# A long-convolution kernel: row turning cut in quarters, two backward steps moved together, bank copies shared with VectorE, loads placed at two points of a slot

## The chip, the cores and the metric

The kernel runs on 1 core of one Trainium2 chip. The metric is device time in microseconds (us) of one launch. Before the change the median of 3 runs is 559.1 us (557.64 to 561.18). The execution that the profiler recorded took 559.32 us; the span from its first to its last instruction is 557.5 us, so 1.8 us lie around the span. All instants below are us from the start of that span.

## What is computed

For one sequence of L = 2048 positions and D = 512 channels, all in float32:

```python
xn = _layernorm(x, axis=-1)
s = _A_ref(xn, ...)                       # a causal long convolution per channel, plus a skip term
g = _silu(_B_ref(xn, w1, b1, w2, b2))     # FFN 512 -> 1792 -> 512 with GELU, then SiLU
return x + s * g
```

`_A_ref` builds a convolution kernel K of length 2048 for each channel from 128 complex modes, and convolves it with the normalised rows by Fourier transforms:

```python
P = jnp.exp(logdA[:, :, None] * l[None, None, :])
K = jnp.einsum("dn,dnl,dn->dl", Cc, P, dB).real
...
y = irfft2(rfft2(up) * rfft2(Kp))[..., :L] + u * Dskip
```

## The kernel before

**Two phases.** The first phase (until 408.32 us) holds the layer norm, both FFN matrix products (each operand split in a high and a low part, three products each), and the generation of the convolution kernels. Its order is the long string `ORDER`, and the change does not reorder it. Nearly all of the change lies in the second phase, the convolution. Its order is written out by hand too: for each of 4 blocks of 128 channels (`b` = 0 to 3) the function `slot(b, g)` is called for `g` = 0 to 7. Every engine takes its instructions strictly in the order in which `slot` and its callees issue them; nothing reorders them later.

**One block.** A transform of 2048 points is taken as 32 by 64.

- `first_dft(b, u, h, gs)` (line 879, matmul L887) is the first forward step of half `h` of the channels, for the rows (`u` = 0) or the convolution kernel (`u` = 1). It writes four PSUM banks. Each of its 64 matrix instructions in the trace is small. `first_out` (L893) copies the four banks into the tile `X` of the next block.
- `second_dft(b, g)` (L907) is the second forward step for 4 of the 32 frequencies, in a PSUM tile of its own tag (two buffers). `spectrum` (L915) copies the rows' half of it to SBUF (`uh`), `product` (L924) multiplies it with the kernel's half, and `combine` (L932, L934, every second slot) makes the complex product `Y` (two buffers).
- `back_dft(b, j)` (L943) is the first backward step for the frequencies of slots 2j and 2j+1. It fills two banks, which `back_out` (L954) copies into `Z`. `turn(b, kh, s)` (L963) transposes a half of `Z` into `T` on VectorE.
- `last_dft` (L983) is the last backward step of a whole block in four banks. `last_out` multiplies with the gate on VectorE (L990) and adds x on GpSimd (L991), and `store` writes four pieces to `out`.

**Banks.** `bank()` hands out four general PSUM banks in turn (two of tag `c`, two of tag `a`). A bank comes free when the copy that reads it is done, so the fifth bank asked for waits for the copy of the first.

**Pipelining between blocks.** While block `b` is in slots 0, 2, 4, 6, its slot also runs the four `first_dft` calls of block `b + 1`: slots 0 and 2 for the rows, 4 and 6 for the kernel. The last parts of a block run in the slots of the next one: the fourth backward step in slot 1, the turns in slots 0 to 4, `last_dft` and `last_out` in slot 5 (slot 4 of the last block).

**The raw rows.** The normalised rows lie in DRAM (`xs`). `side_piece` (L837) loads them for block `b + 2` in four pieces into the tile `raw`; the elements come with the channel innermost. `side_turn` (L856) copies `raw` to `in` with the channel outermost. It does so in two halves on ScalarE in slot 7, one before `spectrum` and one between `spectrum` and `back_out`. `raw`, turned rows and kernel rows share one tag of two buffers, so the kernel rows of block `b + 1` (`kernel_load`, `kernel_half`, L872, two halves of 512 KB) can be loaded once the raw rows are turned; before the change they come at the ends of slots 0 and 1. `side_skip` adds the skip term to each half on GpSimd (L877) before `first_dft(.., 1, ..)` reads it in slots 4 and 6.

**Loads.** All loads of this phase go out on SyncE, in order. `pace` (L799) is a small memset on VectorE into the tile to be loaded; the load waits for it, so a load starts no sooner than VectorE reaches that point of its order. `tail_load` (L972) brings a quarter of the gate and of x.

**The end.** After the loop the last backward step and `last_dft` of block 3 run in halves; for each half of the positions VectorE multiplies (L1145, L1148), one engine adds x (L1149), and two stores go out (L994).

## Time and profile before

| what | value |
|---|---|
| median of 3 runs | 559.1 us (557.64 to 561.18) |
| profiled execution | 559.32 us, span 557.5 us, mean granted TensorE clock 0.989 |
| busy: TensorE matmul, VectorE, ScalarE, GpSimd | 534.6, 454.1, 401.0, 279.8 us |
| first phase | 0 to 408.32 us |
| blocks 0, 1, 2, 3 | from 408.32, 439.72, 478.34, 516.19 us |
| after the loop | 545.19 to 557.5 us |
| moved by DMA | 85.89 MB, mean 154 GB/s |

How to read it: a row of the timeline gives the start and the length in us, the engine, the line, the operation, the names `out<-in`, the size, and how many instructions were merged into the row; in brackets stands the idle time of that engine ahead of it and what ended it. Successive matmuls overlap, so the time that a group really takes is read from its start to the start of the next group. A row of the windows view gives a stretch, its length, the busy time and instruction count of TensorE matmul, weight load, VectorE, ScalarE and GpSimd, then the granted share of the TensorE clock, the busy share of the DMA engines and GB/s.

### The profile page before, as it was taken

The page shows a single profiled execution, that of the slowest core. Times are in us where ns is not written, and L with a number is a line of the kernel's source. Part 1 is how long each engine was busy: PE and PEld are TensorE (multiplying, and loading weights), DVE is VectorE, ACT ScalarE, POOL GpSimd, SP SyncE. Part 2 cuts the span into 40 slices and gives each one's busy share as a digit, 9 for nine tenths or more (in the row PEclk, how much of TensorE's full clock was granted, in tenths as well). Part 3 has the DMA queues.
Part 4 walks back from the last instruction along what each step waited for, and adds up shares of the span by engine and source line. Part 5 has one row for each costly group of instructions (what it writes and reads, how often), then busy time and mean ns, then how long its engine had stood idle before and what let it go on. Part 6 is the DMA issues. An engine that isn't in the chain of part 4 may idle for free.

```text
span 557.5 us, 17629 instructions
## 1 busy us (share of the span) xinstructions
PE 534.6 (96%) x7511; PEld 427.4 (77%) x7511; DVE 454.1 (81%) x720; ACT 401.0 (72%) x580; POOL 279.8 (50%) x383
## 2 busy tenths in 40 slices
PE   8898999999999999999999999999999999999993
PEld 7666777778777777777777777777789887898971
DVE  6899999999999789998897876897453666466996
ACT  3687998799977999869798787799265752743430
POOL 5657389459776579969843484463110003003032
PEclk9999999999999999999999999999998999899998
DMA  8946535835292264834249126442468275362552
GB/s 223 301 151 218 174 127 171 259 127 195 57 325 92 84 220 107 292 105 104 40 133 295 54 91 92 133 115 95 163 232 172 61 236 72 108 200 77 164 198 101
DMA packets 88396, 85.89 MB, mean 154 GB/s; under 512 B 42263, under 2 KB 65051, under 8 KB 87293
## 3 DMA queue, kind: packets, MB, share of 16 engines
q1 hardware_dynamic: 79248, 66.40, 40.2%
q0 software_dynamic: 8768, 17.83, 10.5%
q8 instruction: 59, 0.97, 0.7%
q10 hardware_dynamic: 300, 0.53, 0.3%
q14 instruction: 21, 0.16, 0.1%
HBM read 51.18 MB, written 33.55 MB: 152 GB/s over the span
## 4 chain that ended last, share of the span: by engine, by line
PE 72%; DVE 19%; issue 3%; ACT 2%; DMA 1%; POOL 1%; DVEq 0%; ACTq 0%; SPq 0%; POOLq 0%
PE s L907 10%; PE z L287 8%; PE z L288 7%; PE z L289 7%; PE f L248 7%; PE f L250 7%; PE f L249 7%; PE s L887 6%; PE sa L943 5%; PE kg L655 5%; PE ph L591 2%; DVE hl L274 2%; DVE ra L605 2%; DVE e L644 2%; DVE e L640 1%
## 5 line engine op out<-in xcount | busy, mean ns | idle before, releaser
L617 POOL TENSOR_TENSOR mm<-mm,rc 128x32 f32<-128x32 f32 (+4 forms) x150 | 115.0, 766 | 11.8
L287 PE MATMUL z<-w2h,hh 128*128 128x512 f32 x224 | 97.8, 437 | 0.0
L248 PE MATMUL f<-xh,w1h 128*128 128x512 f32 x220 | 91.4, 415 | 0.0
L289 PE MATMUL z<-w2h,hl 128*128 128x512 f32 x224 | 88.5, 395 | 0.3 <-DVE hl L274 0.3
L250 PE MATMUL f<-xh,w1l 128*128 128x512 f32 x220 | 87.1, 396 | 1.7 <-DVE w1l L233 1.7
L288 PE MATMUL z<-w2l,hh 128*128 128x512 f32 x224 | 88.6, 396 | 0.0
L249 PE MATMUL f<-xl,w1h 128*128 128x512 f32 x220 | 86.7, 394 | 0.0
L924 DVE TENSOR_TENSOR t<-s,uh 128x512 f32<-128x512 f32 x64 | 41.0, 682 | 42.3 <-ACT uh L915 42.0
L907 PE MATMUL s<-X,mc 64*64 64x128 f32 x1536 | 63.7, 282 | 0.1
L274 DVE TENSOR_TENSOR hl<-hf,hh 128x512 fp32r<-128x512 f32 x56 | 53.2, 954 | 4.4 <-ACT hh L268 4.4
L614 POOL COPY mm<-rc 128x32 f32<-128x32 f32 x30 | 13.3, 443 | 78.1 <-DVE e L647 53.4
L907 PEld LDWEIGHTS s<-X,mc 64*64 64x64 f32 x1536 | 47.8, 138 | 5.5 <-DVE t L924 1.7
L250 PEld LDWEIGHTS f<-xh,w1l 128*128 128x128 f32 x220 | 41.3, 188 | 12.8 <-DVE w1l L233 3.0
L262 ACT ACTIVATE hf<-f,b1s 128x512 f32<-128x512 f32 x56 | 38.2, 688 | 17.7 <-DVE hl L274 10.1
L289 PEld LDWEIGHTS z<-w2h,hl 128*128 128x128 f32 x224 | 42.1, 188 | 11.0 <-DVE hl L274 1.1
L287 PEld LDWEIGHTS z<-w2h,hh 128*128 128x128 f32 x224 | 42.5, 190 | 10.3 <-issue 1.0
L605 DVE SCALAR_TENSOR_TENSOR ra<-ra,ph 128x512 f32<-128x512 f32 x64 | 43.6, 681 | 8.3 <-ACT ra L599 7.3
L248 PEld LDWEIGHTS f<-xh,w1h 128*128 128x128 f32 x220 | 41.5, 189 | 9.4 <-issue 0.3
L288 PEld LDWEIGHTS z<-w2l,hh 128*128 128x128 f32 x224 | 42.3, 189 | 8.2 <-DVE w2l L233 0.2
L249 PEld LDWEIGHTS f<-xl,w1h 128*128 128x128 f32 x220 | 41.4, 188 | 9.1
L640 DVE TENSOR_TENSOR e<-mm,ra 128x1024 f32<-128x1024 f32 x32 | 42.9, 1341 | 5.0 <-ACT ra L628 2.6
L893 ACT COPY X<-s 128x512 f32<-128x512 f32 x52 | 27.1, 597 | 25.0 <-PE s L887 25.0
(184 smaller groups left out, 1160.5 us busy)
## 6 DMA issues: line engine op xcount, KB each, us to landing
x<-in_A_u_dram SPq DMA_DIRECT2D x8, 512.0 KB
xs<-x SPq DMA_DIRECT2D x8, 512.0 KB
xt_h<-xh POOLq DMA_DIRECT2D x4, 1024.0 KB, 5.5
xt_l<-xl POOLq DMA_DIRECT2D x4, 1024.0 KB, 7.5
kgd<-ko SPq DMA_DIRECT2D x32, 128.0 KB
za<-zo SPq DMA_DIRECT2D x4, 1024.0 KB
xh<-xt_h POOLq DMA_DIRECT2D x4, 1024.0 KB, 6.1
xl<-xt_l POOLq DMA_DIRECT2D x4, 1024.0 KB, 9.9
```

What stands on the lines that cost most here:

```text
L248: PE.matmul(p, wh[:, k, :], xh[:, k, :], start=(k == 0), stop=False)
L249: PE.matmul(p, wh[:, k, :], xl[:, k, :], start=False, stop=False)
L250: PE.matmul(p, wl[:, k, :], xh[:, k, :], start=False, stop=(k == KD - 1))
L274: V.tensor_sub(hl, hf, hh)
L287: PE.matmul(z, hh[:, s], wh, start=(f0 == 0 and not rows), stop=False)
L288: PE.matmul(z, hh[:, s], wl, start=False, stop=False)
L289: PE.matmul(z, hl[:, s], wh, start=False, stop=(f0 == FA - 1))
L605: V.scalar_tensor_tensor(ra[:, 0, c], ra[:, 1, c], MAGIC, p, op0=ALU.subtract, op1=ALU.subtract)
L617: GP.tensor_mul(mv[:, :, 0:3:2, w:2 * w], mv[:, :, 0:3:2, 0:w], rc[:, 2 + 2 * i:4 + 2 * i, :].rearrange("p j c -> p c j").unsqueeze(3).to_ ...
L640: V.tensor_mul(e1, m1.unsqueeze(1).to_broadcast([P, 2, CH, N1]), ra[:, :, :, :N1])
L907: PE.matmul(p[ka * 64:(ka + 1) * 64, r, o, :, jj], w, xf[b][h, c, :, k, :], start=(c == 0), stop=(c == 1), skip_group_check=True)
L924: V.tensor_mul(t, p[:, i, :, 1].unsqueeze(1).to_broadcast([P, 2, 2, P]), uh)
```

## The change

1. `side_turn` works in quarters of the channels instead of halves. For block `b + 2` quarter 0 stands in slot 7 of block `b` ahead of `spectrum`, quarter 1 in the same slot behind `back_out`, quarters 2 and 3 in slots 0 and 1 of the next block, behind that slot's copies. The two calls outside the loop copy four quarters in one go.
2. `back_dft` of a middle block (1, 2): the second one moves from slot 6 to slot 7, the third one from slot 7 to slot 1 of the next block, where it stands directly ahead of the fourth. `back_out` now stands right behind `spectrum`.
3. `first_out`: VectorE takes two of the four bank copies in every even slot of block 0 (before: none) and in slots 4 and 6 of blocks 1 and 2 (before: slot 4 alone), and one in slots 0 and 2 of blocks 1 and 2 (before: none). VectorE's copies stand behind `product`.
4. Loads stand at two places of a slot (`loads(b, g, 0)` ahead of `product`, `loads(b, g, 1)` at the end), by a table. The kernel rows move from slots 0 and 1 to slots 2 and 3, the tails from slots 0, 1, 2 to places in slots 0, 1, 2, and the raw rows keep slots 3 to 5.
5. The first turn of blocks 0 to 2 moves from slot 7 to slot 0 of the next block, the second from slot 0 to slot 1. In the last block a turn moves from slot 3 to slot 2, and `last_out` of block 2 moves ahead of `product`.
6. At the end, in each half of the positions GpSimd adds one half of the channels and VectorE the other (before: GpSimd both in the first half of the positions, VectorE both in the second).

```diff
--- before.py
+++ after.py
@@ -843,16 +843,16 @@
 
     raws = {}
 
-    def side_turn(b, hs=(0, 1), eng=A):
+    def side_turn(b, qs=range(4), eng=A):
         if b not in raws:
             if b:
                 t = SB["pf"].tile([P, DB, N2], F32, tag="in", name=f"in0_{b}", bufs=2)
             else:
                 t = wka.tile([P, DB, N2], F32, tag="xl", name="in0_0", bufs=2)
-            raws[b] = side[b].rearrange("p m d -> p d m")
+            raws[b] = t, side[b].rearrange("p m d -> p d m")
             side[b] = [[t[:, :DB // 2], t[:, DB // 2:]]]
-        for h in hs:
-            d, r = side[b][0][h], raws[b][:, h * DB // 2:(h + 1) * DB // 2]
+        for q in qs:
+            d, r = (t[:, q * DB // 4:(q + 1) * DB // 4] for t in raws[b])
             A.copy(d, r) if eng is A else eng.tensor_copy(d, r)
 
     def kernel_load(b):
@@ -862,7 +862,7 @@
         else:
             k = [wka.tile([P, DB // 2, N2], F32, tag="x", name=f"in1_0_{h}", bufs=2) for h in range(2)]
         side[b].append(k)
-        for h in range(2 if b < 2 else 0):
+        for h in range(2 if b < 2 else 1):
             kernel_half(b, h)
 
     def kernel_half(b, h):
@@ -887,10 +887,11 @@
                 PE.matmul(p[:, i, :], src[r, 2 * i:2 * i + 2, :], fc[r], start=True, stop=True, skip_group_check=True)
         fp[b, u, h] = list(zip(gs, ps))
 
-    def first_out(b, u, h, engs=(A, A, A, A)):
-        for n, (g, p) in enumerate(fp.pop((b, u, h))):
-            d, p = xf[b][:, :, u, :, 16 * g + 8 * h:16 * g + 8 * h + 8], p.rearrange("p i (c k) -> p c k i", c=2)
-            A.copy(d, p) if engs[n] is A else engs[n].tensor_copy(d, p)
+    def first_out(b, u, h, engs=(A, A, A, A), only=None):
+        for n, (g, p) in enumerate(fp[b, u, h]):
+            if only in (None, engs[n]):
+                d, p = xf[b][:, :, u, :, 16 * g + 8 * h:16 * g + 8 * h + 8], p.rearrange("p i (c k) -> p c k i", c=2)
+                A.copy(d, p) if engs[n] is A else engs[n].tensor_copy(d, p)
 
     sp, sm, yy = {}, {}, {}
 
@@ -993,44 +994,78 @@
     def store(b, t, q):
         q.dma_start(out[b, t], gx[b][1][:, t * TB:(t + 1) * TB].rearrange("p q m -> p (q m)"))
 
+    def loads(b, g, late):
+        def tails(b, *ts):
+            for t in ts:
+                tail_load(b, t)
+
+        def raw(n):
+            if n == 0:
+                side[b + 2] = SB["pf"].tile([P, N2, DB], F32, tag="in", name=f"raw{b + 2}", bufs=2)
+            side_piece(b + 2, n)
+
+        if b == 0:
+            plan = {(1, 0): lambda: mc_load(2), (1, 1): lambda: ct_load(1), (2, 0): lambda: mc_load(3),
+                    (4, 1): lambda: ct_load(2), (6, 1): lambda: ct_load(3)}
+        elif b < NB - 1:
+            plan = {(0, 1): lambda: tails(b - 1, 0), (1, 0): lambda: tails(b - 1, 1), (1, 1): lambda: tails(b - 1, 2),
+                    (2, 0): lambda: kernel_load(b + 1), (2, 1): lambda: tails(b - 1, 3),
+                    (3, 0): lambda: kernel_half(b + 1, 1)}
+        else:
+            plan = {(0, 1): lambda: tails(b - 1, 0), (1, 0): lambda: tails(b - 1, 1), (1, 1): lambda: tails(b - 1, 2),
+                    (2, 0): lambda: tails(b - 1, 3)}
+            plan.update({(g, 1): lambda g=g: tails(b, g - 2) for g in range(2, 6)})
+        if b + 2 < NB:
+            order = ((3, 0), (3, 1), (4, 0), (5, 0)) if b == 0 else ((3, 1), (4, 0), (4, 1), (5, 0))
+            plan.update({k: lambda n=n: raw(n) for n, k in enumerate(order)})
+        if b == NB - 1 and b not in gx and g == 2:
+            big = SB["pf"].tile([P, 2, N1, P], F32, tag="X0", name="last")
+            gx[b] = big[:, 0, :NQ], big[:, 1, :NQ]
+        plan.get((g, late), lambda: None)()
+
     def slot(b, g):
         nxt = b + 1 < NB
         last = not nxt
         i = g // 2
-        sa = {3: (b, 0), 5: (b, 1), 7: (b, 2)}
+        sa = {3: [(b, 0)], 5: [(b, 1)], 7: [(b, 2)]}
         if b:
-            sa[1] = b - 1, 3
-        if b and nxt:
-            sa[6] = sa.pop(5)
-        sa = sa.get(g)
+            sa[1] = [(b - 1, j) for j in ((2, 3) if b > 1 else (3,))]
+            if nxt:
+                sa[7] = sa.pop(5)
+        sa = sa.get(g, [])
         end = b and g == 5 - last
         if b and nxt and g == 4:
             turn(b - 1, 1, 1)
         if last and g == 6:
             turn(b, 0, 0)
         second_dft(b, g)
-        if b + 2 < NB and g == 3:
-            side[b + 2] = SB["pf"].tile([P, N2, DB], F32, tag="in", name=f"raw{b + 2}", bufs=2)
-            side_piece(b + 2, 0)
-        if sa:
-            back_dft(*sa)
+        for k in sa:
+            back_dft(*k)
         if end:
             py = [bank(f"y{b - 1}_{n}").rearrange("p e m -> p (e m)") for n in range(G)]
             last_dft(b - 1, 0, py)
             last_dft(b - 1, 1, py)
-        if nxt and g % 2 == 0:
+        first = nxt and g % 2 == 0
+        if first:
+            engs = (A, A, V, V) if b == 0 or g > 2 else (A, A, A, V)
             first_dft(b + 1, i // 2, i % 2, range(G))
-        turning = b + 2 < NB and g == 7
-        if turning:
+        if b + 2 < NB and g == 7:
             side_turn(b + 2, (0,))
         spectrum(b, g)
-        if turning:
+        for k in sa:
+            back_out(*k)
+        if first:
+            first_out(b + 1, i // 2, i % 2, engs, A)
+        if b + 2 < NB and g == 7:
             side_turn(b + 2, (1,))
-        if sa:
-            back_out(*sa)
-        if nxt and g % 2 == 0:
-            first_out(b + 1, i // 2, i % 2, (A, A, V, V) if b and g == 4 else (A, A, A, A))
+        if nxt and b and g < 2:
+            side_turn(b + 1, (2 + g,))
+        if last and end:
+            last_out(b - 1, py)
+        loads(b, g, 0)
         product(b, g)
+        if first:
+            first_out(b + 1, i // 2, i % 2, engs, V)
         if last and g > 5:
             js = slice(2 * g - 12, 2 * g - 10)
             combine(b, 3, 1, js)
@@ -1038,40 +1073,19 @@
         elif g % 2:
             combine(b, i, 1)
             combine(b, i, 0)
-        if end:
+        if nxt and end:
             last_out(b - 1, py)
-        if g == 7:
-            turn(b, 0, int(last))
-        if b and g == 0:
-            turn(b - 1, 0, 1)
-        if b and g == 2:
-            turn(b - 1, 1, 0)
-        if last and g == 3:
+        if last and g == 7:
+            turn(b, 0, 1)
+        if b and g < 3:
+            turn(b - 1, *((0, 0), (0, 1), (1, 0))[g])
+        if last and g == 2:
             turn(b - 1, 1, 1)
-        if b and nxt:
-            if g == 0:
-                kernel_load(b + 1)
-            if g < 2:
-                kernel_half(b + 1, g)
+        loads(b, g, 1)
         if nxt and g == 3:
             side_skip(b + 1)
-        if b and g < (3 if nxt else 2):
-            for t in range(NTB)[(slice(0, 1), slice(1, 2), slice(2, 4))[g] if nxt else slice(2 * g, 2 * g + 2)]:
-                tail_load(b - 1, t)
-        if last and 1 < g < 6:
-            if g == 2:
-                big = SB["pf"].tile([P, 2, N1, P], F32, tag="X0", name="last")
-                gx[b] = big[:, 0, :NQ], big[:, 1, :NQ]
-            tail_load(b, g - 2)
-        if b == 0:
-            if g in (0, 2):
-                mc_load(2 + g // 2)
-            if g in (2, 4):
-                mc_turn(1 + g // 2)
-            if g in (1, 3, 6):
-                ct_load((1 + g) // 2)
-        if b + 2 < NB and 2 < g < 6:
-            side_piece(b + 2, g - 2)
+        if b == 0 and g in (2, 4):
+            mc_turn(1 + g // 2)
         if b and g == 7 - last:
             for t in range(NTB):
                 store(b - 1, t, SY)
@@ -1146,7 +1160,7 @@
                 else:
                     gp, yp = (t.rearrange(r, i=N1) for t, r in ((gv, "p q (g i) -> p g q i"), (wide[n][:, :, :2 * P], "p g (q i) -> p g q i")))
                     V.tensor_mul(gp, yp, gp)
-                (V if s else GP).tensor_add(xv, gv, xv)
+                (V if n else GP).tensor_add(xv, gv, xv)
             for t in range(2 * s, 2 * s + 2):
                 store(b, t, (SY, A)[t % 2])
     pz.close()
```

## Prediction

> **What bounds the kernel now.** I began with the busy shares of the page.
>
> ```profile
> PE 534.6 (96%) x7511; PEld 427.4 (77%) x7511; DVE 454.1 (81%) x720; ACT 401.0 (72%) x580; POOL 279.8 (50%) x383
> ```
>
> TensorE (PE) is busy for 96%, so an edit that moves work from ScalarE to VectorE wins nothing by itself. It wins only where TensorE waits, or runs slowly, because of it. The first phase keeps its order, so I asked for the busy time of blocks 0, 1 and 2.
>
> ```profile
> 408.32:439.72 31.40, 30.88 (x866) 28.75 (x865) 13.96 (x31) 18.72 (x34) 2.67 (x6) 0.95 0.71 184
> 439.72:478.34 38.62, 36.24 (x963) 31.44 (x961) 23.89 (x44) 20.00 (x34) 5.39 (x6) 1.00 0.55 139
> 478.34:516.19 37.85, 37.09 (x963) 32.64 (x961) 24.75 (x42) 18.31 (x32) 5.54 (x6) 0.95 0.35 114
> ```
>
> TensorE (first busy figure) is idle for 2.4 us of block 1 and under 0.8 us of blocks 0 and 2. Busy time hides slow matmuls, though, so the timeline of TensorE is read by starts, first where nothing disturbs it, then at the conspicuous places.
>
> ```profile
> 422.25 2.06 PE L943 MATMUL sa<-tcn,Y 64*128 64x128 f32 x32
> 424.23 0.67 PE L907 MATMUL s<-X,mc 64*64 64x128 f32 x16
> ...
> 426.14 2.01 PE L887 MATMUL s<-fc,in 32*128 32x64 f32 x64
> 428.08 0.67 PE L907 MATMUL s<-X,mc 64*64 64x128 f32 x16
> ...
> 441.62 0.44 PE L887 MATMUL s<-fc,in 32*128 32x64 f32 x4
> 442.94 2.48 PE L887 MATMUL s<-fc,in 32*128 32x64 f32 x60 [0.88 <-ACT Z L954]
> 445.35 0.67 PE L907 MATMUL s<-X,mc 64*64 64x128 f32 x16
> ...
> 469.06 2.51 PE L943 MATMUL sa<-tcn,Y 64*128 64x128 f32 x32
> 471.50 3.02 PE L887 MATMUL s<-fc,in 32*128 32x64 f32 x64
> 474.45 0.67 PE L907 MATMUL s<-X,mc 64*64 64x128 f32 x16
> ...
> 480.25 0.44 PE L887 MATMUL s<-fc,in 32*128 32x64 f32 x4
> 481.22 2.48 PE L887 MATMUL s<-fc,in 32*128 32x64 f32 x60 [0.54 <-ACT Z L954]
> 483.63 1.11 PE L907 MATMUL s<-X,mc 64*64 64x128 f32 x16
> ```
>
> From start to start, an undisturbed backward step takes 1.98 us (422.25 to 424.23), a second forward step 1.91, a first forward step 1.94. In slot 0 of block 1 the first forward step takes 441.62 to 445.35 = 3.73, so **1.79 are lost**; in slot 0 of block 2 480.25 to 483.63 = 3.38, **1.44 lost**. In slot 6 of block 1, backward and first forward step take 469.06 to 474.45 = 5.39 instead of 3.92, 1.47 lost. The row at 483.63 shows matmuls that are slow without waiting (1.11 instead of 0.67 us); the windows view gives the clock there and at one other place.
>
> ```profile
> 418.85:422.26 3.41, 3.41 (x66) 3.08 (x63) 0.06 (x1) 1.93 (x4) 0.00 (x0) 0.50 0.85 253
> 483.70:487.12 3.42, 3.42 (x65) 3.20 (x64) 1.21 (x4) 1.89 (x4) 0.00 (x0) 0.50 0.32 86
> ```
>
> In two stretches of 3.41 us the granted clock is 0.50, which loses 1.7 us each. A last kind of loss names no engine:
>
> ```profile
> 459.50 2.01 PE L887 MATMUL s<-fc,in 32*128 32x64 f32 x64
> ...
> 463.41 0.33 PE L907 MATMUL s<-X,mn 64*64 64x128 f32 x2 [1.09 <-issue]
> ```
>
> The second of these rows stands behind 1.09 us for which the profile shows no releaser; the first is the forward step of slot 4, needed below.
>
> **The change part by part.** The sum is made against the profiled execution, 559.32 us (span 557.5), which stands 0.2 us above the median of 559.1.
>
> **Quarters and `back_out` (removes 3.2).** In slot 0 the first forward step asks for the two banks of the backward step ahead of it, and these wait for ScalarE:
>
> ```profile
> 440.38 2.02 ACT L856 COPY in<-raw 128x1024 f32<-128x1024 f32 x1
> 442.28 1.09 ACT L954 COPY Z<-sa 128x512 f32<-128x512 f32 x2
> ```
>
> The half turn of 2.02 us stands ahead of the 1.09 us of bank copies. A quarter takes half of it, some 1.0 us. In the new order, `back_out` starts when the backward step ends, 0.1 us after the 439.72 at which the next group starts, and is done by 441.0, ahead of the 441.62 at which the banks are wanted. Quarter 1 follows until 442.0. The first half of the forward step reads quarter 0 alone, and in the built program the wait for quarter 1 stands in the middle of that step, at 441.62 + 0.97 = 442.6. So nothing is late next in slot 0: −1.79 −1.44 = −3.2. Quarters 2 and 3 are 1.0 us each on ScalarE in slots 0 and 1, behind the copies; they push `uh` of slots 1 and 2 by some 0.5 us, and `product` frees a buffer that TensorE asks for only two slots later. That cover, a slot of 3.85 us, makes them free; so are four copies for two outside the loop, under TensorE's products of the first phase.
>
> **The backward steps (adds 0.4).** Each is only moved, 1.98 us on TensorE wherever it stands. In slot 6 the first forward step now follows the second forward step directly and wants four banks at 469.06. VectorE frees them with
>
> ```profile
> 468.18 2.48 DVE L990 TENSOR_TENSOR gb<-y,gb 128x512 f32<-128x512 f32 x4
> ```
>
> so the fourth bank is free at 470.66, and the step loses about 1.65 us instead of 1.47. That is +0.2 in each of blocks 1 and 2 (bounds 0 to +0.4 each). In slot 1 of blocks 2 and 3, two backward steps want four banks. In block 2 ScalarE frees three of them in 1.5 us behind slot 0's forward step, and VectorE's one is due only behind the first backward step; the second forward step (1.91 us) covers all of it. Without the cover it would be 0.6 us. In slot 7, `combine` now waits for a backward step that reads its buffer; TensorE ends that about when VectorE arrives, 0.
>
> **Bank copies on VectorE (0).** Copies of two banks take VectorE 1.3 us; they stand behind `product`, and the banks are wanted a slot later. VectorE has 3.85 us a slot and is at 24 of 38 us in block 1.
>
> **Loads (adds 0.4).** The first kernel half moves from slot 0 to slot 2, while its reader stays in slot 4.
>
> ```profile
> 446.71 0.33 SPq L872 DMA_DIRECT2D in<-kgd  x1
> ```
>
> ```profile
> 452.65 0.23 POOL L877 TENSOR_TENSOR in<-in,dsk 128x16 f32<-128x16 f32 x1 [39.72 <-DMA in<-kgd]
> ```
>
> From issue to GpSimd's add it took 5.9 us. Now the point of issue lies behind the combine and a turn of slot 1 on VectorE:
>
> ```profile
> 449.99 0.69 DVE L932 TENSOR_TENSOR Y<-t,t 128x512 f32<-128x512 f32 x1
> ...
> 453.15 1.23 DVE L963 STREAM_TRANSPOSE T<-Z 128x1024 f32<-128x1024 f32 x1
> ```
>
> The combine ends at 450.68; less the 1.79 us that slot 0 saves, plus some 0.5 for quarter 2 ahead of `uh`, plus the turn of 1.23, this is 450.6. The two loads of a tail quarter stand ahead on SyncE, some 0.4 us each, so the issue is at about 451.4. With 5.9 us and the add of 0.23 the rows are ready at 457.5. TensorE wants them at 459.50 − 1.79 = 457.7, or 0.6 earlier if the unnamed wait ahead of it is gone. I take +0.4, between 0 (4.3 us of landing, quoted below) and +2 (the two tail loads first, at half of 4.3 us). Block 2 gives 2 us more room, by its second backward step. The memset ahead of this load waits for quarter 3, and behind it on VectorE stands `product` of slot 2, whose `uh` comes later on ScalarE anyway: 0. Raw rows: 0, they are wanted in slot 7.
>
> **The clock (removes 1.7).** The second half-rate stretch follows the 1.44 us wait of block 2, which goes; I let that stretch go with it, and keep the first, which follows an unnamed wait. Bounds: 0 and −3.4. The Trainium skill, "TensorE: Matmul & The Clock Gate", section "What's actually happening", has the clock halved after a whole idle window of about 3.4 us. This trace disagrees: the idle time ahead of 483.63 is 0.54 us. By that rule the change would leave the clock alone, and the sum would be 1.7 us higher.
>
> **The end (adds 0.2).**
>
> ```profile
> 548.93 3.03 POOL L1149 TENSOR_TENSOR last<-last 128x512 f32<-128x512 f32 x2 [10.69 <-DVE last L1148]
> ```
>
> ```profile
> 550.14 0.69 DVE L1149 TENSOR_TENSOR last<-last 128x512 f32<-128x512 f32 x1
> 550.75 0.75 DVE L1145 TENSOR_TENSOR last<-y,last 128x256 f32<-128x256 f32 x2
> 551.53 0.97 DVE L1149 TENSOR_TENSOR last<-last 128x512 f32<-128x512 f32 x1
> ```
>
> GpSimd's two adds take 3.03 us, and VectorE's second add 0.97 instead of 0.69: adds of the two engines hold each other up. In the new order they meet in both halves. If one waits for the other's end, and a lone GpSimd add takes 1.24, then: multiplications from 548.20 to 549.4, GpSimd's add to 550.2, VectorE's to 550.9, multiplications to 551.6, GpSimd to 552.85, VectorE's to 553.55. That is 1.05 later than now (552.50), but half the bytes have left by then, and the transfer shown at the end (1 MB in some 2.9 us) is halved, −1.4 at most, if the queues drain at once. I take +0.2; −1.0 if the adds don't meet, +1.0 if nothing is saved on the transfer. The Trainium skill, "SBUF — State Buffer", section "SBUF: two separate sides", speaks against this edit: the port pair that VectorE and GpSimd share is an exclusive lock held for a whole instruction. The rows agree (3.03, 0.97); without that rule the sum would be 1.2 lower.
>
> **Last block (0).** The moved turn frees TensorE of a wait of 0.2 us at its last backward step, and `last_out` ahead of `product` costs VectorE about the same later.
>
> **Unnamed waits (0).** Like that of 1.09 us; where they fall among moved loads I can't tell. Taken as equal, bounds −2 and +2.
>
> Sum: −3.2 + 0.4 + 0.4 − 1.7 + 0.2 = −3.9, so 559.3 − 3.9 = **555.4 us**.
>
> **The rivals.**
>
> *The clock stays.* Both half-rate stretches stay, wherever they fall: 555.4 + 1.7 = 557.1. For it: the first one follows no wait that the change touches. Against it: the second stands right behind one.
>
> *More goes than I count.* Both stretches go, and the adds of the end don't meet: 555.4 − 1.7 − 1.2 = 552.5. For it: VectorE and GpSimd may start in a kinder order; against it: 3.03 and 0.97 us.
>
> *The kernel half comes late (slower).* The place is slot 4 of blocks 1 and 2. If the half moves only when the tail quarter ahead of it is through, at 5.9 + 4.3 = 10.2 us after its issue (4.3 is what the second half takes below), TensorE waits some 4.0 us in block 1 and 3.7 in block 2, of which 0.4 is counted: 555.4 + 7.3 = 562.7. It decides from about 5.5 us after the issue in block 1, and about 6.5 in block 2. Against it:
>
> ```profile
> 450.73 0.32 SPq L872 DMA_DIRECT2D in<-kgd  x1
> ```
>
> ```profile
> 455.02 0.23 POOL L877 TENSOR_TENSOR in<-in,dsk 128x16 f32<-128x16 f32 x1 [2.14 <-DMA in<-kgd]
> ```
>
> with tails around it, 4.3 us were enough.
>
> *The change doesn't do what it says.* The quarters only move the wait: if quarter 1 is late and slot 0 still waits 1.5 us in each block, 555.4 + 3.0 = 558.4. Against it: 0.6 us of room by the sum above.
>
> **How the numbers follow.** Forecast 0.45; the clock stays 0.19; more goes 0.19; a late kernel half 0.11; the wait stays 0.06. Over 1% of 559.1 us is 5.6 us, about what a measurement of this kernel can tell from no change: faster means below 553.5, slower above 564.7. Faster: the case "more goes" and a twentieth of the forecast's, by unnamed waits, 0.24. Slower: a part of the late half together with unnamed waits, 0.08. The rest, 0.68, is within 1%. The range reaches from 551.5 (552.5 less half the bound of the unnamed waits) to 560.0, above the kept wait and the kept clock, and leaves out most of the late half (0.1) and the best of "more goes" (0.07).
>
> **What would show it.** In slot 0 of blocks 1 and 2 the first forward step takes 1.9 to 2.1 us from start to start, and its wait for L954's copies is gone. In slot 6 it waits for L990 instead, about 1.65 us. In slot 4 of block 1 it waits 0 to 1 us for GpSimd's L877 add. At most one stretch of 0.50 remains ahead of the end. At the end VectorE's and GpSimd's adds of x follow each other, and the last stores are issued about 6 us after the last turn instead of 4.5. I am wrong if slot 0 still waits for ScalarE, if slot 4 waits for over 2 us, or if unnamed waits grow by over 2 us.

## The result

The changed kernel takes 555.11 us (median; 550.06 to 560.51) beside 560.57 us (556.29 to 563.68) for the kernel before on the same chip: a ratio of 0.9896, 95% interval 0.987 to 0.9922, so 1.0% faster. The profiled execution takes 553.42 us (span 551.6, mean granted clock 0.996) against 559.32. The medians are over all runs, the ratios here and below over the fast ones (within 1.5% of a kernel's fastest), which leaves out three of the 20 runs of the changed kernel and none of the kernel before; over all runs the two medians stand at 0.990. The forecast was 555.4.

**Profile after.** From the page of the changed kernel, the busy shares:

```profile
span 551.6 us, 17643 instructions
PE 530.1 (96%) x7511; PEld 424.0 (77%) x7511; DVE 462.4 (84%) x736; ACT 394.0 (71%) x570; POOL 281.3 (51%) x385
```

ScalarE's work moved to VectorE (454.1 to 462.4 us), and TensorE has the same share as before: again nothing can be read from shares alone. The windows view of the changed kernel, for blocks 0 to 3 (columns as in the prediction):

```profile
407.72:437.96 30.24, 29.92 (x865) 27.49 (x865) 20.18 (x41) 14.81 (x27) 2.69 (x6) 1.00 0.75 186
437.96:473.98 36.02, 33.32 (x931) 28.89 (x929) 26.41 (x49) 16.90 (x28) 5.42 (x6) 1.00 0.60 141
473.98:508.69 34.71, 34.32 (x962) 30.44 (x960) 26.48 (x45) 16.99 (x29) 5.41 (x6) 1.00 0.39 126
508.69:539.34 30.65, 29.86 (x802) 26.32 (x800) 26.94 (x47) 11.79 (x22) 4.99 (x4) 1.00 0.59 189
```

Block 0 took 31.40 us before and takes 30.24; block 1 38.62 and 36.02, of which 1.98 is a backward step that now stands in block 2; block 2 37.85 and 34.71 (one such step in, one out); block 3 29.00 and 30.65, with one more step. The first phase is 0.60 shorter. The clock column shows 1.00 in all four blocks; the two half-rate stretches of before are gone. Now TensorE's timeline of the changed kernel in slot 0 of blocks 1 and 2 and slot 1 of block 2:

```profile
439.87 0.89 PE L887 MATMUL s<-fc,in 32*128 32x64 f32 x22
441.25 1.44 PE L887 MATMUL s<-fc,in 32*128 32x64 f32 x42 [0.49 <-issue]
442.62 0.67 PE L908 MATMUL s<-X,mc 64*64 64x128 f32 x16
...
475.89 2.01 PE L887 MATMUL s<-fc,in 32*128 32x64 f32 x64
477.83 0.67 PE L908 MATMUL s<-X,mc 64*64 64x128 f32 x16
...
479.74 3.84 PE L944 MATMUL sa<-tcn,Y 64*128 64x128 f32 x64
483.51 0.67 PE L908 MATMUL s<-X,mc 64*64 64x128 f32 x16
```

In block 2 the first forward step takes 477.83 − 475.89 = 1.94 us, its undisturbed time; it was 3.38. In block 1 it takes 2.75 instead of 3.73. What is left, 0.81, names no engine and stands behind matmul 22 of 64, while the waits for ScalarE's copies stood behind the fourth and sixth. Two backward steps in a row take 3.77, a little under twice 1.98. Slots 4 to 6 of block 1 and slot 6 of block 2, same view:

```profile
454.25 0.67 PE L908 MATMUL s<-X,mc 64*64 64x128 f32 x16
...
457.47 2.01 PE L887 MATMUL s<-fc,in 32*128 32x64 f32 x64 [1.24 <-POOL in L877]
459.42 0.67 PE L908 MATMUL s<-X,mc 64*64 64x128 f32 x16
...
460.87 0.33 PE L908 MATMUL s<-X,mn 64*64 64x128 f32 x2 [0.58 <-issue]
...
467.15 0.84 PE L887 MATMUL s<-fc,in 32*128 32x64 f32 x6
468.16 1.99 PE L887 MATMUL s<-fc,in 32*128 32x64 f32 x58 [0.17 <-DVE gb L991]
470.09 0.67 PE L908 MATMUL s<-X,mc 64*64 64x128 f32 x16
...
501.19 0.92 PE L887 MATMUL s<-fc,in 32*128 32x64 f32 x4
...
502.88 1.99 PE L887 MATMUL s<-fc,in 32*128 32x64 f32 x58 [0.17 <-DVE gb L991]
504.80 0.67 PE L908 MATMUL s<-X,mc 64*64 64x128 f32 x16
```

Slot 4 of block 1 has a new wait. The second forward step before it ends its turn at 454.25 + 1.91 = 456.16, the first forward step starts at 457.47: 1.3 lost for GpSimd's addition to the kernel's first half. Slot 6 waits for VectorE's gate multiplications, as forecast: 470.09 − 467.15 − 1.94 = 1.00 lost in block 1 and 1.67 in block 2.

**Where the time went.** The profiled executions differ by 5.9 us. By starts, against the undisturbed times, the parts are (from unrounded starts, so a last digit can differ by 0.01 from a difference of printed ones):

| part | before, lost | after, lost | difference |
|---|---|---|---|
| slot 0, waits for ScalarE's copies | 1.79 + 1.45 | 0 | −3.2 |
| half-rate clock ahead of the end | 1.62 + 1.66 | 0 | −3.3 |
| slot 6 of blocks 1 and 2 | 1.46 + 1.49 | 1.00 + 1.67 | −0.3 |
| two backward steps in a row, twice | 0 | −0.2 each | −0.4 |
| slot 4 of block 1, kernel's first half | 0 | 1.30 | +1.3 |
| last block, named waits | 0.49 | 0.87 | +0.4 |
| waits without a name | 0.94 + 0.60 + 1.51 + 0.51 | 0.47 + 0.47 + 0.34 + 0.81 + 0.99 + 0.63 | +0.2 |
| first phase | 408.32 | 407.72 | −0.6 |
| from the last turn's end to the span's end | 9.2 | 9.2 | −0.1 |

The sum is −6.0, 0.1 off. (The first phase ends between 406.8 and 409.0 us in the profiles of all kernels here, so its −0.6 may be chance.) One execution is not the mean, though: averaged over all runs, (1 − granted clock) × span is 6.4 us before (26 and 29 runs in two groups) and 5.3 after (20 runs). The clock is worth −1.1 on average, give or take 1.3 (95%), not the −3.3 of this pair. In every profile 1.8 to 3.7 us of this loss lie behind the last matmul (2.8 before, 2.4 after), where TensorE has nothing left to do.

### The profile page after: what moved, and what is told of

The parts are those of the page before. It is cut to its first block, busy times and chain, and to the rows that moved or that the text cites. A ratio compares the mean times of both kernels' runs of the same rounds, so it can differ in the third digit from the quotient of the medians.

```text
span 551.6 us, 17643 instructions
## 1 busy us (share of the span) xinstructions
PE 530.1 (96%) x7511; PEld 424.0 (77%) x7511; DVE 462.4 (84%) x736; ACT 394.0 (71%) x570; POOL 281.3 (51%) x385
## 4 chain that ended last, share of the span: by engine, by line
PE 68%; DVE 22%; issue 4%; ACT 3%; DMA 2%; POOL 1%; DVEq 0%; ACTq 0%; POOLq 0%
PE s L908 10%; PE z L287 7%; PE z L288 7%; PE z L289 7%; PE f L248 6%; PE f L250 6%; PE s L887 6%; PE f L249 6%; PE sa L944 5%; PE kg L655 4%; DVE hl L274 2%; PE ph L591 2%; DVE ra L605 2%; DVE e L644 2%; DVE e L647 2%
## 5 line engine op out<-in xcount | busy, mean ns | idle before, releaser
L617 POOL TENSOR_TENSOR mm<-mm,rc 128x32 f32<-128x32 f32 (+4 forms) x150 | 116.3, 776 | 11.8
L908 PE MATMUL s<-X,mc 64*64 64x128 f32 x1536 | 61.0, 273 | 0.3 <-issue 0.2
L274 DVE TENSOR_TENSOR hl<-hf,hh 128x512 fp32r<-128x512 f32 x56 | 51.7, 926 | 4.6 <-ACT hh L268 4.6
L908 PEld LDWEIGHTS s<-X,mc 64*64 64x64 f32 x1536 | 45.4, 133 | 5.8 <-issue 2.7
L640 DVE TENSOR_TENSOR e<-mm,ra 128x1024 f32<-128x1024 f32 x32 | 42.6, 1331 | 4.8 <-POOL pr_h L522 2.5
L644 DVE TENSOR_TENSOR e<-mm,ra 128x1024 f32<-128x1024 f32 x32 | 44.6, 1393 | 0.0
```

The lines of the kernel that those rows point to most:

```text
L274: V.tensor_sub(hl, hf, hh)
L617: GP.tensor_mul(mv[:, :, 0:3:2, w:2 * w], mv[:, :, 0:3:2, 0:w], rc[:, 2 + 2 * i:4 + 2 * i, :].rearrange("p j c -> p c j").unsqueeze(3).to_ ...
L640: V.tensor_mul(e1, m1.unsqueeze(1).to_broadcast([P, 2, CH, N1]), ra[:, :, :, :N1])
L644: V.tensor_mul(e2[:, :, :, :H], m2[:, :, :H].unsqueeze(1).to_broadcast([P, 2, CH, H]), ra[:, :, :, dn])
L908: PE.matmul(p[ka * 64:(ka + 1) * 64, r, o, :, jj], w, xf[b][h, c, :, k, :], start=(c == 0), stop=(c == 1), skip_group_check=True)
```

## The experiments

Single runs of one kernel spread by some 2 us around their mean (up to 4 in run e), so the interval of a ratio is ±0.3 to 0.45% and most experiments here cannot be told apart by their times alone. The waits in their profiles can. "Ratio" is to the kernel before, on the same chip; the kernel before differs by up to 1.5 us from one comparison to the next, so ratios are compared and not medians. The profiles of a (560.98 us), b (560.78) and l (557.73) are of executions well above their medians.

| run | starts from | median, us | ratio | 95% interval |
|---|---|---|---|---|
| a quarters alone | before | 555.89 | 0.9948 | 0.9916 to 0.998 |
| k order alone | before | 556.87 | 0.9949 | 0.9915 to 0.9983 |
| b whole turn in slot 7 | after | 555.25 | 0.9925 | 0.9895 to 0.9954 |
| f backward steps as before | after | 556.45 | 0.9936 | 0.9908 to 0.9964 |
| g copies on ScalarE | after | 555.09 | 0.9926 | 0.9892 to 0.9961 |
| c kernel half first | after | 553.32 | 0.9887 | 0.9842 to 0.9931 |
| d end as before | after | 554.54 | 0.9915 | 0.988 to 0.9949 |
| e raw rows in long pieces | after | 555.03 | 0.9884 | 0.9841 to 0.9926 |
| i no raw transfer, filled | after | 556.82 | 0.9946 | 0.9912 to 0.998 |
| l no raw transfer, no fill | after | 553.75 | 0.988 | 0.9837 to 0.9924 |
| h last_out early | c | 553.62 | 0.9887 | 0.9846 to 0.9927 |
| j h, and the end in a new order | h | 552.14 | 0.9853 | 0.9818 to 0.9888 |

The theory: slot 0's waits for ScalarE go (−3.2) and the clock follows, a late kernel half gives some back. The rivals: the gain comes from other parts (backward steps, VectorE's copies), or from waits that only moved.

### Slot 0: the quarters, or the order (a, k, b)

Run a is the kernel before with the turn in quarters (the numbers in the call are now quarters) and `back_out` behind `spectrum`, the kernel's loads one slot later:

```diff
-        if turning:
-            side_turn(b + 2, (1,))
         if sa:
             back_out(*sa)
+        if turning:
+            side_turn(b + 2, (1,))
...
+        if b and nxt and g < 2:
+            side_turn(b + 1, (2 + g,))
...
-            if g == 0:
+            if g == 1:
                 kernel_load(b + 1)
-            if g < 2:
-                kernel_half(b + 1, g)
+            if 0 < g < 3:
+                kernel_half(b + 1, g - 1)
```

> The kernel before with part 1 alone: the raw rows are turned in quarters (slot 7 twice, slots 0 and 1 once), back_out stands behind spectrum, and the kernel halves are loaded one slot later because their buffer is the raw rows'. All bank copies stay on ScalarE as before, and so do the backward steps. Theory (ScalarE's half turn of 2.02 us stood ahead of the bank copies): the first forward step of slot 0 takes 1.9 to 2.2 us in blocks 1 and 2 instead of 3.73 and 3.38, slot 6 still loses 1.5 us in each, and the time is 3 us below the kernel before, 4 to 5 if half-rate stretches go with the waits. Rival (the gain comes from taking copies off ScalarE): slot 0 still loses over 1 us in each block, and the time is within 1 us of the kernel before.

Slot 0 loses nothing in either block. Slot 6 loses what it lost before (0.46 + 1.01 and 0.48 + 1.01). The ratio says −2.9 us of 559.1 (interval −1.1 to −4.7), about the 3.2 of slot 0.

Run k tells cutting from order: halves as before, and only `back_out` moved ahead of the second half's turn.

```diff
-        if turning:
-            side_turn(b + 2, (1,))
         if sa:
             back_out(*sa)
+        if turning:
+            side_turn(b + 2, (1,))
```

> The kernel before with its order in slot 7 alone changed: the backward step's copy stands ahead of the turn of the second half of the raw rows, which is not cut into quarters. The prediction put 3.2 us on quarters and copy together. Theory (the order is what counts: the first forward step of slot 0 reads the first half only): slot 0 of blocks 1 and 2 loses 0 to 0.3 us instead of 1.79 and 1.45, and the time is that of the quarters alone, 555.5 to 557. Rival (the cut is needed: the bank copies of slot 0 stand behind the whole turn on ScalarE, so the second forward step of slot 1 or the first of slot 2 comes late): 1 us or more is lost in slots 0 to 2 of each block, 557.5 to 560.

ScalarE's timeline around the end of block 0, then TensorE's in slot 0 of blocks 1 and 2, all of run k:

```profile
438.59 1.07 ACT L954 COPY Z<-sa 128x512 f32<-128x512 f32 x2
439.55 2.05 ACT L856 COPY in<-raw 128x1024 f32<-128x1024 f32 x1
```

```profile
439.58 2.12 PE L887 MATMUL s<-fc,in 32*128 32x64 f32 x64
441.64 0.67 PE L907 MATMUL s<-X,mc 64*64 64x128 f32 x16
...
475.98 2.01 PE L887 MATMUL s<-fc,in 32*128 32x64 f32 x64
477.92 0.67 PE L907 MATMUL s<-X,mc 64*64 64x128 f32 x16
```

The copies are done as the first forward step begins, and it takes 2.06 and 1.94 us: 0.12 and 0 lost. The half turn of 2.05 us goes on beside it and hurts nobody, since the step of slot 0 reads the other half; the steps of slots 1 and 2 lose nothing either. The ratio is that of run a. So the order removes the wait; cutting the turn in quarters adds nothing that a run here shows. In time this is half of the change's gain: 0.9949 beside 0.9896.

Run b goes the other way: the changed kernel with all four quarters in slot 7, two ahead of `spectrum` and two ahead of `back_out`.

```diff
-            side_turn(b + 2, (0,))
+            side_turn(b + 2, (0, 1))
         spectrum(b, g)
+        if b + 2 < NB and g == 7:
+            side_turn(b + 2, (2, 3))
```

> The changed kernel with part 1 undone: all four quarters in slot 7, two ahead of spectrum and two between spectrum and back_out, as the halves stood before. Theory: slot 0 of blocks 1 and 2 loses 1.4 to 1.8 us again by the wait for L955's copies, and the time is 3 to 4 us above the changed kernel. Rival (VectorE's share of the copies makes the room, the quarters nothing): slot 0 loses under 0.5 us, and the time is within 1 us of the changed kernel.

ScalarE's timeline of run b at the end of block 0, and TensorE's step behind it:

```profile
444.81 2.13 ACT L856 COPY in<-raw 128x512 f32<-128x512 f32 x2
446.85 1.06 ACT L955 COPY Z<-sa 128x512 f32<-128x512 f32 x2
```

```profile
447.11 2.85 PE L887 MATMUL s<-fc,in 32*128 32x64 f32 x64
449.88 0.67 PE L908 MATMUL s<-X,mc 64*64 64x128 f32 x16
```

The wait comes back, but at 0.84 us in block 1 and 0.68 in block 2, half of what was expected. The turn starts 447.11 − 444.81 = 2.3 us ahead of the step, where before it was 441.62 − 440.38 = 1.2: ScalarE is 1.1 us earlier. That VectorE's bank copies give it this lead is a reading of the order; no run takes both parts out. The time did not rise by the 3 to 4 us expected: the ratios, 0.9925 and 0.9896, stand 1.6 us apart, about the 1.5 of the two waits, and their intervals overlap.

### The backward steps and VectorE's copies (f, g)

```diff
-            sa[1] = [(b - 1, j) for j in ((2, 3) if b > 1 else (3,))]
+            sa[1] = [(b - 1, 3)]
             if nxt:
-                sa[7] = sa.pop(5)
+                sa[6] = sa.pop(5)
```

> The changed kernel with part 2 undone: the backward steps of blocks 1 and 2 stand in slots 6 and 7 again, and one stands in slot 1. Theory (moving them is worth nothing: the wait for last_out's multiplications only goes from the backward step to the first forward step): slot 6 loses 1.4 to 1.6 us over both steps in each block, the time is within 1 us of the changed kernel, if anything lower by 0.4. Rival (two steps side by side give ScalarE room): slot 0 waits for L955's copies again, 0.5 us or more in each block, and the time is 1 to 2 us higher.

With the steps at their old places slot 6 loses 0.08 + 1.13 in block 1 and 0.48 + 1.01 in block 2, together 2.7, as much as the changed kernel's 1.00 + 1.67. Slot 0 stays free of waits. The third backward step's place is neutral in slot 6. The time is another matter: the median is 1.3 us higher, in the rival's range though slot 0 does not wait, and the ratios (0.9936 and 0.9896) have intervals that overlap by little. This profile has 4.0 us of unnamed waits in block 0, so whether the move of the steps is worth something outside slot 6 stays open.

```diff
-            engs = (A, A, V, V) if b == 0 or g > 2 else (A, A, A, V)
+            engs = (A, A, V, V) if b and g == 4 else (A, A, A, A)
```

> The changed kernel with part 3 undone: ScalarE makes all bank copies but two in slot 4 of blocks 1 and 2. Theory (with the quarters in place these copies stand beside TensorE's work): slot 0 of blocks 1 and 2 loses under 0.3 us, slot 1 of block 2 under 0.6, and the time is within 1 us of the changed kernel. Rival (the copies on VectorE carry part of the gain, as slot 0 lost only 0.8 and 0.7 us with the whole turn in slot 7): ScalarE comes late, the steps of slots 1, 2 or 6 lose 2 us more in all, and the time is 2 us higher.

Without VectorE's extra copies slot 0 still loses nothing, slot 6 loses 1.67 in both blocks, and the median is the changed kernel's (by ratio it is 0.3% higher, within the intervals). No wait returned, so that term of 0 stands as far as these runs tell.

### The kernel's first half (c)

In the changed kernel, SyncE's timeline ahead of slot 4 of block 1, and GpSimd's addition:

```profile
449.89 0.42 SPq L973 DMA_DIRECT2D xb<-in_u_rows_dram  x1
450.40 1.50 SPq L872 DMA_DIRECT2D in<-kgd  x1
```

```profile
457.19 0.23 POOL L877 TENSOR_TENSOR in<-in,dsk 128x16 f32<-128x16 f32 x1 [44.83 <-DVE raw L799]
```

The half is asked for at 450.40, behind a tail quarter's two pieces (the gate's and, shown, that of x), and added to at 457.19. Run c asks for it ahead of that tail:

```diff
-            plan = {(0, 1): lambda: tails(b - 1, 0), (1, 0): lambda: tails(b - 1, 1), (1, 1): lambda: tails(b - 1, 2),
-                    (2, 0): lambda: kernel_load(b + 1), (2, 1): lambda: tails(b - 1, 3),
+            plan = {(0, 1): lambda: tails(b - 1, 0), (1, 0): lambda: tails(b - 1, 1), (1, 1): lambda: kernel_load(b + 1),
+                    (2, 0): lambda: tails(b - 1, 2), (2, 1): lambda: tails(b - 1, 3),
```

> The changed kernel with the first kernel half issued at the end of slot 1, ahead of the third tail quarter, which takes its place in slot 2. Theory (the half waits in the queue for the tail quarter ahead of it): the wait of 1.24 us for GpSimd's add in slot 4 of block 1 falls below 0.4 us, and the time by about 1 us. Rival (the half is late because VectorE reaches its place late): it is issued only some 0.9 us earlier, the wait stays above 0.8 us.

GpSimd's and TensorE's timelines of run c at that place:

```profile
453.49 0.62 POOL L877 TENSOR_TENSOR in<-in,dsk 128x16 f32<-128x16 f32 x1 [41.51 <-DMA xb<-in_u_rows_dram]
```

```profile
455.11 2.01 PE L887 MATMUL s<-fc,in 32*128 32x64 f32 x64
457.05 0.67 PE L908 MATMUL s<-X,mc 64*64 64x128 f32 x16
```

The half is there 1.0 us ahead of need (454.11 against 455.11), and the step loses nothing. Two things add up: in run c the half is asked for 1.9 us earlier (448.46), and its last piece lands 4.9 us behind that instead of 6.5. In the changed kernel that piece lands at 456.90, 0.3 us ahead of the addition, so the memset that the row above names is most likely not what GpSimd waited for. The longer landing is not shown to come from the tail: with the tail directly ahead it takes 4.0 to 6.5 us (runs b, d, e, f, g, i, l and the changed kernel), without it 4.2 to 4.9 (c, h, j). The ratio falls from 0.9896 to 0.9887, 0.5 us, with intervals that overlap; the time does not show the 1.3 us.

### The end (d)

```diff
-                (V if n else GP).tensor_add(xv, gv, xv)
+                (V if s else GP).tensor_add(xv, gv, xv)
```

> The changed kernel with part 6 undone: at the end GpSimd adds x in both channel halves of the first positions and VectorE in both of the second. Theory (the adds of VectorE and GpSimd wait for each other's end): the last stores are issued 4.3 us after the last turn ends instead of 5.1, the first ones 3.7 instead of 2.6; the stretch from the last turn to the end of the span changes by less than 0.5 us, since half the bytes then leave later. Rival (the split shortens the end as it is): the end is 0.5 to 1 us longer than in the changed kernel.

The changed kernel's timeline of VectorE and GpSimd behind the last turn (which ends at 542.43), then run d's (541.63):

```profile
543.08 1.27 POOL L1163 TENSOR_TENSOR last<-last 128x512 f32<-128x512 f32 x1 [11.27 <-DVE last L1162]
543.64 1.26 DVE L1163 TENSOR_TENSOR last<-last 128x512 f32<-128x512 f32 x1
...
546.26 1.20 DVE L1163 TENSOR_TENSOR last<-last 128x512 f32<-128x512 f32 x1
```

```profile
542.29 3.03 POOL L1163 TENSOR_TENSOR last<-last 128x512 f32<-128x512 f32 x2 [11.27 <-DVE last L1162]
...
544.90 0.97 DVE L1163 TENSOR_TENSOR last<-last 128x512 f32<-128x512 f32 x1
```

In the changed kernel VectorE's add starts while GpSimd's runs and ends some 0.6 us after it: 1.26 and 1.20 us, where one alone takes 0.69. The last add ends 547.46 − 542.43 = 5.0 us behind the last turn; in run d it is 545.87 − 541.63 = 4.2. But the span ends at 551.6 and 550.8, 9.2 us behind the last turn in both, and in the kernel before (557.5 − 548.27) as well: earlier first stores (2.5 us behind the last turn instead of 3.7 in run d) give back about what the later adds cost.

The Trainium skill, "SBUF — State Buffer", section "SBUF: two separate sides", says that VectorE and GpSimd share a port pair under a lock held for a whole instruction. These rows agree: VectorE's add is not interleaved with GpSimd's but done 0.55 us after its end (543.08 + 1.27 = 544.35, 543.64 + 1.26 = 544.90), a little less than the 0.69 of an add alone.

### Waits without a name (e, i, l)

In before, after and most runs TensorE stops in blocks 0 and 1 with no releaser, from kernel to kernel behind the same matmuls (number 58 of slot 2's first step of block 0, numbers 19 to 21 of the second steps of slots 4 to 6 of block 1), for 0.3 to 3 us. Raw rows are loaded in slots 3 to 5 of these two blocks. (Not all the waits fit that: slot 2 of block 0 comes ahead of the raw rows, and run k loses 1.14 and 1.06 us in blocks 2 and 3, where none are loaded.) Run e reads other data, which lies in rows of 8 KB, in place of the raw rows of blocks 2 and 3:

```diff
+        if b > 1:
+            SY.dma_start(t[g * N1:(g + 1) * N1].rearrange("n m d -> n (m d)"), ux[b, g].rearrange("(n r) m -> n (r m)", n=N1))
+            return
```

> The changed kernel, but the raw rows of blocks 2 and 3 are read from a part of x that lies in rows of 8 KB: the same places in the order, the same 256 KB a piece, other data, in packets of up to 8 KB instead of 128 bytes. It leaves out that blocks 2 and 3 convolve the normalised rows. Theory (TensorE's unnamed waits are for its instructions, whose loads queue behind the many small packets of the raw rows): the unnamed waits of blocks 0 and 1, some 4 us in the profile of the changed kernel and up to 9 in the one of the quarters alone, fall below 1.5 us, and the time by 2 to 4 us. Rival (any transfer delays them, or none does): they stay above 3 us, and the time is within 1 us of the changed kernel.

Block 0 lost nothing without a name, block 1 still 1.81 and 1.18; the time is the changed kernel's. The expected fall came in one block of two, and the 3.0 us that are left are nearer to the rival's value. Run i leaves the transfer for block 3 out (and with it that block's own data), GpSimd fills the rows:

```diff
+        if b == NB - 1:
+            GP.memset(t[g * N1:(g + 1) * N1], 0.0)
+            return
```

> The changed kernel with the raw rows of block 3 set to zero by GpSimd in place of their transfer; this leaves out that block 3 convolves its own rows, and takes the four transfers out of slots 3 to 5 of block 1. TensorE's waits without a name stand in the changed kernel in blocks 0 and 1 (1.4 and 2.4 us), where raw rows are loaded, and nowhere in block 2, where none are. Theory (TensorE's instructions come late while that transfer holds the queues): in slots 3 to 6 of block 1 less than 0.5 us is left of the waits without a name, the 1.24 us for the kernel's first half in slot 4 goes too, block 0 keeps 1 us or more, and the time is 1 to 3 us under that of the changed kernel (552 to 554). Rival (the waits belong to a place in the order of instructions, whatever the queues carry): block 1 keeps 1.5 us or more of them, and only the wait for the kernel's half goes, 554 to 555.

TensorE's timeline of run i, slot 4 of block 1, and the windows view of what follows:

```profile
457.54 2.84 PE L890 MATMUL s<-fc,in 32*128 32x64 f32 x64 [1.66 <-POOL in L880]
```

```profile
458.52:465.35 6.83, 6.83 (x136) 5.42 (x129) 2.04 (x6) 1.66 (x3) 5.41 (x4) 0.50 0.01 4
```

Block 1 lost nothing without a name, as the theory had it; block 0 lost 0.6, where the theory had 1 or more. But the fill stood ahead of GpSimd's addition (1.66 us), and two half-rate stretches of 6.83 and 3.41 us followed, so the time tells nothing. Run l has neither transfer nor fill:

```diff
+        if b == NB - 1:
+            return
...
-            raws[b] = t, side[b].rearrange("p m d -> p d m")
+            raws[b] = t, dsk[:, b].unsqueeze(2).to_broadcast([P, DB, N2]) if b == NB - 1 else side[b].rearrange("p m d -> p d m")
```

> The changed kernel without the transfer of the raw rows of block 3, and with nothing put in their place: the turn of that block reads a small table that lies in SBUF, repeated, so block 3 convolves other data than it should and everything else stays. In the run that had GpSimd fill the rows, block 1 lost nothing without a name, but the fill stood ahead of GpSimd's addition to the kernel's half (1.7 us of TensorE's time) and two half-rate stretches of 10.2 us followed. Theory (the transfer costs the block its unnamed waits and the late half): slots 3 to 6 of block 1 lose under 0.5 us without a name and under 0.3 us on the kernel's half, block 0 still has its unnamed waits, and the time is 1.5 to 3 us under that of the changed kernel, 552 to 553.6. Rival (that run's waits were moved by the fill, not taken away by the missing transfer): block 1 keeps 1.5 us or more without a name, time 554 to 556.

TensorE's timeline of run l, slot 5 of block 1:

```profile
461.57 0.67 PE L910 MATMUL s<-X,mc 64*64 64x128 f32 x16
...
463.65 0.33 PE L910 MATMUL s<-X,mn 64*64 64x128 f32 x2 [1.21 <-issue]
```

The wait of slot 5 is there, 1.62 us, without any raw transfer in the block; slots 4 and 6 are free, and the kernel's half is not late. The time, 553.75, lies between the theory's range and the rival's, and the theory's condition (under 0.5 us) failed. And run j, below, has the transfer and loses nothing without a name in slots 3 to 6 of block 1. So the theory falls: the transfer of raw rows neither suffices for these waits nor is it needed.

The traces do show what these waits go with. The page lists a queue named `q8 instruction`, which brings packets of 16 KB. In the blocks of all fourteen kernels there are 45 waits of over 0.15 us without a releaser. They stand at every 127th or 128th matmul or a multiple of that, and each ends 1.2 to 1.9 us after such a packet has landed, while the packets come 3.2 to 7.9 us apart. Ahead of matmul 4806 of the program, for example, the changed kernel waits 0.49 us and goes on 1.31 us after the landing; the kernel before, whose packet landed 3.45 us ahead of that matmul, does not wait. So TensorE most likely stands still until its next instructions are there, and the size is how late the packet is. No run changes how instructions are brought, so this is not shown, and what delays a packet stays open.

### Slot 6, and a version that beats both (h, j)

Run h takes run c and moves `last_out` ahead of `product` between blocks, so that VectorE frees the four banks first:

```diff
-        if last and end:
+        if end:
             last_out(b - 1, py)
...
-        if nxt and end:
-            last_out(b - 1, py)
```

> A version that should beat both: the changed kernel with the first kernel half ahead of the third tail quarter, and with last_out ahead of product in blocks 1 and 2 as it stands in the last block. Theory: VectorE frees the four banks 2.5 us earlier, and the first forward step of slot 6 loses 0.6 to 0.8 us instead of 1.65 in each block; with the kernel half 2.5 to 3 us in all below the changed kernel. Rival (product and combine come 2.5 us later, and TensorE waits for them in slot 7 or 0): the gain of slot 6 is lost there, and the time is within 1 us of the changed kernel.

Slot 6 of block 2 loses 0.67 instead of 1.67, but the backward step of slot 7 then takes 0.87 us longer, and the median stays at run c's: the rival's case. Run j adds a new order at the end: GpSimd makes one of the four adds, VectorE three.

```diff
+        times(0, 0)
+        plus(0, 0, GP)
+        times(0, 1)
+        times(1, 0)
+        plus(0, 1, V)
+        for t in range(2):
+            store(b, t, (SY, A)[t % 2])
+        times(1, 1)
+        plus(1, 0, V)
+        plus(1, 1, V)
+        for t in range(2, 4):
+            store(b, t, (SY, A)[t % 2])
```

> The changed kernel with three edits: the next block's kernel rows are asked for one place earlier, the last step's multiplications and additions stand ahead of the spectrum's product in slot 7 also between blocks, and at the end GpSimd makes one of the four additions and VectorE three, each half's stores behind its own two. Theory: slot 4 of block 1 waits for no kernel half (1.2 us less), slot 6 of block 2 loses 0.7 instead of 1.67, the first stores are issued 2.7 us and the last 4.65 us after the last turn instead of 2.6 and 5.1: 0.4 us less at the end than the run with the first two edits (553.6), so 552.5 to 553.5, and 6 to 7 us under the kernel before. Rival: the end is set by the transfers, which start no sooner, or unnamed waits take the gain: 553.5 to 555.

TensorE's timeline of run j in slots 6 and 7 of block 1:

```profile
466.75 0.52 PE L887 MATMUL s<-fc,in 32*128 32x64 f32 x6
467.44 1.99 PE L887 MATMUL s<-fc,in 32*128 32x64 f32 x58 [0.17 <-DVE gb L991]
469.36 0.67 PE L908 MATMUL s<-X,mc 64*64 64x128 f32 x16
...
471.27 2.06 PE L944 MATMUL sa<-tcn,Y 64*128 64x128 f32 x32
474.08 0.67 PE L908 MATMUL s<-X,mc 64*64 64x128 f32 x16 [0.76 <-DVE X L894]
```

Slot 6 loses 469.36 − 466.75 − 1.94 = 0.67 here too (1.00 in the changed kernel), and the gain turns into a wait of 0.76 behind slot 7's backward step, for VectorE's bank copies, which now stand behind a later `product`. The end, by VectorE's timeline of run j:

```profile
544.16 0.71 DVE L1165 TENSOR_TENSOR last<-last 128x512 f32<-128x512 f32 x1
...
545.46 1.28 DVE L1165 TENSOR_TENSOR last<-last 128x512 f32<-128x512 f32 x2
```

No add is held up (0.71, and 1.28 for two). The last turn ends at 542.40, the span at 550.9: 8.5 us, 0.7 less than in before, after and run d (8.9 to 9.0 in runs i and l, whose end is the changed kernel's). With the kernel's half in time (c) this is the fastest version, 552.14 us (551.05 to 553.43), a little under its expected range and 1.5% under the kernel before. Against the changed kernel's ratio (0.9896) the intervals overlap, so by how much it beats that one is not settled.

## Why the prediction was right, and where not

The forecast, 555.4, is 0.3 us from the median of 555.11. That it is so close is partly luck: it started from 559.1 to 559.3 and took off 3.9, while the kernel before has a median of 560.57 in this comparison, so the change took off 5.5 (5.9 in the pair of profiles). Its largest step holds; four others are off, partly against each other.

- **Quarters and `back_out`, −3.2: right.** The named waits of slot 0 went from 1.79 and 1.45 to 0; undone in run b, half of them return, and run a alone gives −2.9. The reason was too wide: run k shows that the place of `back_out` does it, and the cut is not needed. The rival that the change does not do what it says (558.4) falls.
- **The backward steps, +0.4: mechanism right, size off.** The wait changed hands from ScalarE to VectorE as said. In block 2 it is 1.67 for the 1.65 forecast; in block 1 it is 1.00, and slot 6 lost 1.49 before in block 2. Together −0.3, and two steps in a row gain another 0.2 each. Run f shows no loss from the move.
- **VectorE's copies, 0: right** (run g). They give slack rather than time.
- **Loads, +0.4: under-sized.** It measured +1.3. The issue was at 450.4 instead of the forecast 451.4, but the addition was done 7.0 us behind it, not 6.1, and TensorE wanted the rows at 456.2 and not at 457.1 to 457.7. The row of before had no tail pieces directly ahead; that they make the landing longer is likely and not shown, as it varies from 4.0 to 6.5 us with them there. The wait lies inside the bounds of 0 and 2, and run c, which only swaps the two, takes it away. The rival of a half that comes 4 us late (562.7) did not happen; block 2 has no such wait.
- **The clock, −1.7: the sign right, the size not settled.** Both stretches are gone from this profile (−3.3), one more than forecast; over all runs it is −1.1, give or take 1.3.
- **The end, +0.2: −0.1.** The adds meet and exclude each other, as the rows of before suggested, and the shorter last transfer pays for it. The forecast times of the last stores, 6 and 4.5 us behind the last turn, were off: the rows give 5.0 and 4.2 to the last add.
- **Last block 0: +0.4; unnamed waits 0: +0.2; the first phase was not counted: −0.6.** The backward step of block 3 waits 0.87 for ScalarE instead of 0.34.

Of the rivals, "more goes" is the nearest to the profiled pair: both half-rate stretches went, but the adds did meet. The prediction's chance of a faster kernel, 0.24, is not what its own terms give (0.19 and a twentieth of 0.45 are 0.21). One line's place is worth about half of the change's effect (run k); the other half no run here pins down, since undoing a single other part (d, f, g) moves the ratio by 0.2 to 0.4%, which is the size of the intervals.

## What to carry to other kernels

When a long copy stands on an in-order engine between a producer and the short copy that frees its bank, move the short copy ahead before cutting the long one: here the order alone took the whole wait away. Where two engines' adds exclude each other, it may pay to give one engine most of them and to interleave other work (in the one profile of run j the end was 0.4 to 0.7 us shorter); check the end by the last landing instead of the last instruction. A wait that is taken from one slot is worth only what the next consumer in order does not ask back: `last_out` early gained 1.0 us in slot 6 and returned most of it a slot later.

## What the runs showed of the hardware that was not expected

- **Half rate after little idle time.** The windows view of run l, the 3.41 us ahead of a half-rate stretch and the stretch itself:

```profile
469.23:472.64 3.41, 3.05 (x71) 2.57 (x64) 2.85 (x5) 0.58 (x1) 3.41 (x3) 1.00 0.00 0
472.64:476.05 3.41, 3.41 (x62) 3.29 (x62) 1.29 (x2) 1.59 (x3) 1.46 (x2) 0.50 0.35 125
```

TensorE's matmuls cover 3.05 of 3.41 us, and the clock is halved all the same. (Busy time hides waits here too: by starts, the first forward step that begins at 469.30 takes 3.72 us instead of 1.94.) The Trainium skill, "TensorE: Matmul & The Clock Gate", section "What's actually happening", asks for a whole idle window; this row disagrees, and in no run here does a half-rate stretch of the blocks follow one. Nor does the same wait always bring it: slot 6 of block 2 lost 1.67 us in after and in run c, and only run c's clock fell (at 502.66). What decides is open. Averaged over a kernel's runs, the loss to the clock was 6.4 to 6.9 us before, 5.3 after, and between 2.9 (h) and 7.3 (i) in the experiments, each with the 1.8 to 3.7 us behind the last matmul in it.
- **Waits with no releaser keep their places.** They stand behind the same matmul of the same step in kernel after kernel, from 0 to 3 us long; taking the raw rows' transfer away leaves some of them, and leaving it in place (run j) does not always bring them. They are as large as most effects measured here. All 45 of them end 1.2 to 1.9 us after a packet of the instruction queue has landed, as told under run l.
